# A new order of steps over five engines, the last experts in column halves, and products of ones ahead of the first queries

## The chip, the cores and the metric

The kernel runs on one core of a Trainium2 chip. The metric is the device time of one execution in microseconds (us), the median of three runs. The profile is one further execution, taken by the hardware profiler.

## The reference

Attention that keeps the 32 largest scores of each row, and behind it a mixture of four experts, all in float32. Batch 2, 8 heads, 576 positions, head width 64; 1152 tokens of width 512; four experts of inner width 1024.

```python
scores = q @ k.T / sqrt(64)
kth = 32nd largest of each row of scores
attn = softmax(where(scores >= kth, scores, -1e9))
x = (attn @ v), heads side by side            # 1152 x 512
p = domain_probs / domain_probs.sum(-1)
out = sum over e of p[:, e] * (relu(x @ w1[e]) @ w2[e])
```

## The kernel before

**Tiles and units.** The tokens are cut into ten tiles t0 to t9 of 128 rows (t0 and t9 have 64 rows). A unit u is one head of a tile (in t0 and t9 one pair of heads): t0 holds u0 to u3, t1 u4 to u11, and so on, eight a tile; t5 holds u36 to u43, t6 u44 to u51, t9 u68 to u71. Every float32 operand of the large products is split into a high and a low float16 half, and a product is three float16 products.

**The way of a unit.** `emit_qk` (L642) makes the scores of a unit in PSUM, in one of two buffers. Seven VectorE steps (`topk_op`, MAX8 at L655 and MATCH_REPLACE8 at L657 and L659) find the 32nd largest score. `emit_nb` (L692, L695) makes the bias of the exponential, `emit_exp` (L699) the exponential on ScalarE, and `emit_mask` drops what is below the threshold, either in one VectorE operation (mode d, L706) or in two on ScalarE and one on GpSimd (mode r, L709, L713, L716). `emit_a` splits the weights into halves (L724 on ScalarE, L726 and L728 on GpSimd), `emit_at` transposes them by a DMA from SP's queue (L734, tile `at`), and `emit_av` (L764) multiplies them with v.

**The way of a tile.** When its units are done, `emit_x_half` normalises (L784 to L788), `x_hi` and `x_lo` split x (L808 on ScalarE, L813 on GpSimd), a DMA transposes it (L816, tile `xt`), and `moe` runs the experts: `m1` (L881 to L883, half an expert's inner width at a time), ReLU and split (`h_hi` L892, `h_lo` L899 and L906, or L902 on VectorE), `m2` (L924), and `evac`, which adds an expert's result into the accumulator `o`, on VectorE (L948) or by ScalarE and GpSimd (L946, L951). The accumulator is stored by one DMA a tile (L955). In t9 experts go in pairs, each on 64 columns of the array, so two matmuls run side by side.

**The start.** Queries of t0 are loaded and transposed (L558), keys transposed (L579), and the first scores are float32 products (L598). `kv_gram` and `w_gram` (L1027, L497) are matmuls from which scales are found; the weights come in sixteen DMAs of 1 MB (`load_w`, L341) and are scaled and split on ScalarE and GpSimd (L526, L532, L535).

**What sets the order.** Every step is registered under an index, and the table `ISSUE` gives each stage of each step its place in one sequence. The five engines execute in exactly that order, so an instruction that waits holds back all that stand behind it on its engine. The strings `H_LO`, `MASKS`, `NB`, `EVAC` and `KV1` choose the engine of single steps (a is ScalarE, d VectorE, p GpSimd, r the mask in three operations). `MASKS` and `NB` have one letter a unit, u0 first.

Of the kernel before, what the change touches and what calls it, by code (L numbers as in the profile page):

```python
# [9 lines left out]
BF16 = mybir.dt.bfloat16  # L10
# [33 lines left out]
H_LO = ('pddd', 'dppppppp', 'pppppppd', 'dpdpppdp', 'dppppppp', 'pppdpdpp', 'pppppdpp', 'pppppppp', 'pppppppp', 'ppdp')  # L44

MASKS = 'ddddddddddddddddrrrrrrrrrrrrrrdrrdrrrrrrrrrdrdrrrrrrrrrrrrrrrrrrrrrrrrrr'
NB = 'aaaapdpadddaaadddddpdddadddpdddpdpapadppppppppaaaaadpppapppaapppppapaapp'
# [6 lines left out]
EVAC = ('dddp', 'dppd', 'dddd', 'dppd', 'ddpp', 'dppp', 'dddd', 'dddd', 'dddd', 'dddd')  # L54
KV1 = dict(k='aaaaaaad', v='aaaaaaaa')
# [1166 lines left out]
```

## Time and profile before

| | us |
|---|---|
| median of three runs | 544.7 |
| lowest and highest | 543.14, 544.88 |
| device time of the profiled execution | 546.72 |
| its span, first to last instruction | 544.9 |
| TensorE busy | 504.1 |
| VectorE busy | 432.0 |
| ScalarE busy | 368.3 |
| GpSimd busy | 366.1 |

The execution falls into a stretch in which VectorE has no gaps and TensorE has many (from about 10 to 110 us), one in which both are nearly full (110 to 310), one in which TensorE is full but for a few waits (310 to 400), one in which it is full (400 to 540), and the 4.9 us behind the last matmul. Busy time of TensorE takes the latency of a matmul in, so gaps below that don't show in it. The granted clock is shown as a share of the full 2.4 GHz; for the first 12 us the profile has no record of it, and the durations of equal instructions tell it there.

### The profile page before, as it was taken

How to read it: one execution, taken by the hardware profiler on the slowest of the kernel's cores; microseconds unless marked ns; L12 is line 12 of the kernel's file. 1: busy time of each engine (PE TensorE's matmuls, PEld its weight loads, DVE VectorE, ACT ScalarE, POOL GpSimd, SP SyncE). 2: the span in 40 equal slices, each digit the busy share in tenths (PEclk: the TensorE clock that was granted, in tenths of full speed). 3: DMA queues.
4: the chain of work that ended last, by engine and by line, in shares of the span. 5: the costliest groups of instructions: out<-in, count | busy, mean ns of one | idle time of the engine just before them, and what ended most of it. 6: DMA issues, size and time to landing. Idle time of an engine off the chain costs nothing.

```text
span 544.9 us, 16191 instructions
## 1 busy us (share of the span) xinstructions
PE 504.1 (93%) x6666; PEld 379.9 (70%) x6666; DVE 432.0 (79%) x965; ACT 368.3 (68%) x604; POOL 366.1 (67%) x404
## 2 busy tenths in 40 slices
PE   5978875699999999999999989999999999999996
PEld 3657754586777677868777767767867686777584
DVE  3999999999999999999999887987897877600111
ACT  2999999998777777688877566666655574234121
POOL 0599999998887767686977666685864764445210
PEclk9977996999999999999999989999999999999999
DMA  7999997543443645655524752354323232201300
GB/s 174 358 260 325 248 298 165 101 92 79 88 93 59 147 76 109 136 93 102 121 68 88 122 89 64 66 72 66 65 45 77 47 69 47 43 2 27 69 4 30
DMA packets 142698, 58.35 MB, mean 107 GB/s; under 512 B 130080, under 2 KB 134304, under 8 KB 142624
## 3 DMA queue, kind: packets, MB, share of 16 engines
q1 hardware_dynamic: 139200, 54.43, 46.9%
q10 hardware_dynamic: 3424, 2.88, 1.7%
q8 instruction: 52, 0.85, 0.6%
q14 instruction: 22, 0.18, 0.1%
HBM read 25.45 MB, written 2.36 MB: 51 GB/s over the span
## 4 chain that ended last, share of the span: by engine, by line
PE 53%; DVE 16%; POOL 9%; DMA 7%; issue 7%; ACT 7%; SPq 1%; POOLq 0%; ACTq 0%; DVEq 0%
PE m L924 23%; DVE m L655 7%; PE m L881 7%; PE m L882 7%; PE m L883 7%; DMA at<-a 4%; DVE w L659 3%; PE ps L642 3%; PE av L764 3%; POOL a L726 3%; DVE w L657 2%; POOL w L716 2%; DVE w L706 1%; POOL h L906 1%; ACT w L699 1%
## 5 line engine op out<-in xcount | busy, mean ns | idle before, releaser
L883 PE MATMUL m<-xt,w 128*128 128x128 f16 (+1 forms) x1280 | 198.8, 215 | 0.5 <-POOL w L535 0.5
L924 PE MATMUL m<-w,h 128*128 128x512 f16 (+1 forms) x960 | 196.0, 379 | 0.2 <-ACT o L943 0.2
L881 PE MATMUL m<-xt,w 128*128 128x128 f16 (+1 forms) x1120 | 177.8, 214 | 1.2 <-DMA xt<-xhl 1.2
L882 PE MATMUL m<-xt,w 128*128 128x128 f16 (+1 forms) x1120 | 177.8, 214 | 0.0
L655 DVE MAX8 m<-w 128x8 f32<-128x576 f32 x216 | 161.2, 754 | 3.1
L924 PEld LDWEIGHTS <-h 128*128 128x128 f16 (+1 forms) x960 | 84.0, 100 | 89.9 <-issue 1.1
L883 PEld LDWEIGHTS <-w 128*128 128x128 f16 x1280 | 123.2, 98 | 0.6 <-POOL w L535 0.6
L881 PEld LDWEIGHTS <-w 128*128 128x128 f16 x1120 | 108.0, 98 | 4.4 <-issue 2.5
L906 POOL TENSOR_TENSOR h<-hf,h 128x512 f16<-128x512 f32 x59 | 68.5, 1161 | 62.4 <-ACT hf L899 57.9
L882 PEld LDWEIGHTS <-w 128*128 128x128 f16 x1120 | 107.7, 98 | 1.8
L659 DVE MATCH_REPLACE8 w<-m,w 128x576 f32<-128x576 f32 x144 | 106.9, 742 | 0.0
L726 POOL TENSOR_TENSOR a<-w,a 128x512 f16<-128x512 f32 x68 | 79.0, 1162 | 31.0 <-ACT a L724 26.1
L716 POOL TENSOR_TENSOR w<-w,d 128x576 f32<-128x576 f32 x52 | 66.7, 1287 | 34.0 <-ACT d L713 30.1
L892 ACT ACTIVATE h<-m 128x512 f16<-128x512 f32 x72 | 42.7, 593 | 61.5 <-PE m L883 40.2
L699 ACT ACTIVATE w<-ps,nb,es 128x576 f32<-128x576 f32 x68 | 56.3, 828 | 31.6 <-DVE m L655 27.3
L655 DVE MAX8 m<-ps 128x8 f32<-128x576 f32 x72 | 54.6, 758 | 27.5 <-PE ps L642 16.5
L948 DVE SCALAR_TENSOR_TENSOR o<-m,pniw,o 128x512 f32<-128x512 f32 (+1 forms) x17 | 12.6, 744 | 62.4 <-PE m L924 51.9
L724 ACT ACTIVATE a<-w 128x576 f16<-128x576 f32 x68 | 45.8, 679 | 19.1 <-POOL w L716 12.9
L657 DVE MATCH_REPLACE8 w<-m,ps 128x576 f32<-128x576 f32 x72 | 53.8, 747 | 0.0
L642 PE MATMUL ps<-kt,qa 128*128 128x288 f16 x128 | 35.5, 296 | 16.5 <-DVE w L706 11.5
L764 PEld LDWEIGHTS <-at 128*128 128x128 f16 (+1 forms) x1008 | 36.3, 100 | 12.9 <-DMA at<-a 7.5
L764 PE MATMUL av<-vt,at 128*128 128x65 f16 (+1 forms) x1008 | 39.5, 195 | 5.6 <-DMA at<-a 5.6
(159 smaller groups left out, 769.3 us busy)
## 6 DMA issues: line engine op xcount, KB each, us to landing
w<-in_moe_w_dram SPq DMA_DIRECT2D x16, 1024.0 KB, 7.7
qraw<-in_q_dram SPq DMA_DIRECT2D x8, 256.0 KB, 3.5
qb<-qa SPq DMA_DIRECT2D x16, 128.0 KB, 2.5
out_dram<-o ACTq DMA_DIRECT2D x8, 256.0 KB, 2.7
at<-a SPq DMA_TRANSPOSE x68, 3.3
vraw<-in_v_dram SPq DMA_DIRECT2D x2, 512.0 KB, 7.8
nraw<-in_v_dram SPq DMA_DIRECT2D x4, 256.0 KB, 3.2
kraw<-in_k_dram SPq DMA_DIRECT2D x4, 256.0 KB, 2.9
```

Source lines behind the costliest of these rows:

```text
L655: DVE.max(m, s_t[u] if r == 0 else w_t[u])
L657: DVE.match_replace(rows2(w_t[u]), m, s_t[u], NEG)
L659: DVE.match_replace(w_t[u], m, w_t[u], NEG)
L699: ACT.activation(rows2(w_t[u]), s_t[u], AF.Exp, bias=nb, scale=es)
L716: POOL.tensor_tensor(w, w, g, op=OP.mult)
L726: POOL.tensor_tensor(a[:, 640:1152], w[:, 0:512], a[:, 0:512], op=OP.subtract)
L764: PE.matmul(o, lhsT=att[:, blk, ps], rhs=r, start=(i == 0), stop=(i == len(seq) - 1))
L881: PE.matmul(o, lhsT=HI[e, 0, c][:, fc], rhs=xs(0, c), start=(c == 0), stop=False)
L882: PE.matmul(o, lhsT=HI[e, 0, c][:, fc], rhs=xs(1, c), start=False, stop=False)
L883: PE.matmul(o, lhsT=LO[e, 0, c][:, fc], rhs=xs(0, c), start=False, stop=(c == 3))
L906: POOL.tensor_tensor(h[:, 1], hf, h[:, 0], op=OP.subtract)
L924: PE.matmul(y[z * 64:z * 64 + M, :], lhsT=h_t[es, qd][:, p // 2, h0:h0 + M], rhs=w, start=(fc == 0 and p == 0), stop=(fc == 7 and p == 2))
```

## The change

Four things are changed.

- The table `ISSUE` is replaced: all steps are the same, their sequence is another one on all engines. 
- The letters of `H_LO`, `MASKS`, `NB`, `EVAC` and `KV1` are others. Of 68 units behind t0, masks in one VectorE operation are 20 instead of 16.
- In t9, `m2` of the last pair of experts goes over the columns in two halves of 256. The first half stays in the bank of `m2`, the second goes to the bank that `av` had. `evac` adds each half by VectorE operations on 256 columns, and each half is stored by a DMA of its own, the first from SP's queue, the second from ScalarE's.
- Ahead of everything else TensorE gets 24 matmuls of ones with ones (bf16, 128 by 128) into the bank `m2`; nothing reads the result.

```diff
-H_LO = ('pddd', 'dppppppp', 'pppppppd', 'dpdpppdp', 'dppppppp', 'pppdpdpp', 'pppppdpp', 'pppppppp', 'pppppppp', 'ppdp')
+H_LO = ('pddd', 'dppppppp', 'ppppdppp', 'dpppppdp', 'dpdpppdp', 'ppppdppd', 'pppppppp', 'pppppppp', 'pppdpppp', 'pppp')
-MASKS = 'ddddddddddddddddrrrrrrrrrrrrrrdrrdrrrrrrrrrdrdrrrrrrrrrrrrrrrrrrrrrrrrrr'
-NB = 'aaaapdpadddaaadddddpdddadddpdddpdpapadppppppppaaaaadpppapppaapppppapaapp'
+MASKS = 'ddddddddddddddddrrdrrrrrrrrdrrrrrrrrrrrdrdrrrrdrrrrdrrdrrrrrrdrrrrrrrrrr'
+NB = 'aaaadddddddaddadddddaadaadaapdddpppapppdpaaapapaaappppppapppppappaaaaaaa'
-EVAC = ('dddp', 'dppd', 'dddd', 'dppd', 'ddpp', 'dppp', 'dddd', 'dddd', 'dddd', 'dddd')
-KV1 = dict(k='aaaaaaad', v='aaaaaaaa')
+EVAC = ('ddpp', 'ddpp', 'dddp', 'ddpp', 'dppp', 'dpdd', 'dddd', 'dddd', 'dddd', 'dddd')
+KV1 = dict(k='aaaaadaa', v='aaaaaaaa')
 ISSUE = [
-    (1,), (9,), (10,), (42,), (48,), (0, 3), (2, 4), (23, 24), (43, 47), (27, 31), (14,), (15, 16), (19, 22, 35, 41),
...
             def m2(es, qd):
                 if qd == 0:
                     y_t[es] = bank(ps_m2, "m2")
+                    if t == tiles[-1] and es[-1] == order[-1]:
+                        y2_t.append(bank(ps_av, "av"))
...
+                    if t == tiles[-1] and es[-1] == order[-1]:
+                        continue
...
+                if t == tiles[-1] and es[-1] == order[-1]:
+                    for hc in (slice(0, 256), slice(256, 512)):
+                        for f in range(4):
+                            fc = qd * 4 + f
+                            for p in range(3):
+                                for z, e in enumerate(es):
+                                    h0 = (4 * z + f) * M
+                                    w = (LO if p == 1 else HI)[e, 1, fc // 2]
+                                    w = w[:, (fc % 2) * 512 + hc.start:(fc % 2) * 512 + hc.stop]
+                                    PE.matmul((y2_t[0] if hc.start else y)[z * 64:z * 64 + M, hc], lhsT=h_t[es, qd][:, p // 2, h0:h0 + M], rhs=w,
+                                              start=(fc == 0 and p == 0), stop=(fc == 7 and p == 2))
...
+                if t == tiles[-1] and es[-1] == order[-1]:
+                    r0 = t[0] * S + t[1]
+                    for hc, zs in ((slice(0, 256), (0,)),) if z == 0 else ((slice(0, 256), (1,)), (slice(256, 512), (0, 1))):
+                        for zz in zs:
+                            DVE.scalar_tensor_tensor(
+                                acc[0][0:M, hc], (y2_t[0] if hc.start else y_t[es])[zz * 64:zz * 64 + M, hc], pniw[0:M, group(t), es[zz]:es[zz] + 1],
+                                acc[0][0:M, hc], op0=OP.mult, op1=OP.add)
+                        if z == 1:
+                            (ACT if hc.start else SP).dma_start(out=out[r0:r0 + M, hc], in_=acc[0][0:M, hc])
+                    yield
+                    yield
+                    return
...
         DVE.memset(ones, 1.0)
         DVE.memset(kraw0[64:128, 4], 0.0)
+        warm = bank(ps_m2, "m2")
+        for _ in range(24):
+            PE.matmul(warm[:, 0:128], lhsT=ones.bitcast(BF16)[:, 0:128], rhs=ones.bitcast(BF16)[:, 0:128], start=True, stop=True)
```

Three places show what the sequence does. The first is SP's queue at the start. `kraw0`, `vraw0`, `qraw` are keys, values and queries, `pn` the probabilities, `w00` and `w10` the first weights of experts 0 and 1, `qa` the transposed queries of t1. Before:

```order
L976 DMA kraw0_143<-in_k_dram 128x4x64 x4
L356 DMA qraw_204<-in_q_dram 128x8x64
L1006 DMA pn_120<-in_moe_domain_probs_dram 128x4x4
...
L341 DMA w00_123<-in_moe_w1_dram 128x2x1024 x2
...
L341 DMA w10_125<-in_moe_w1_dram 128x2x1024 x2
L393 DMA_TRANSPOSE qa_440<-qhl_206 128x8x128
```

And of the change:

```order
L1004 DMA kraw0_143<-in_k_dram 128x4x64 x4
L357 DMA qraw_254<-in_q_dram 128x8x64
L342 DMA w00_123<-in_moe_w1_dram 128x2x1024
L1037 DMA pn_120<-in_moe_domain_probs_dram 128x4x4
...
L342 DMA w00_123<-in_moe_w1_dram 128x2x1024
...
L342 DMA w10_125<-in_moe_w1_dram 128x2x1024
L394 DMA_TRANSPOSE qa_398<-qhl_258 128x8x128
L342 DMA w10_125<-in_moe_w1_dram 128x2x1024
```

The first half of `w00` moves ahead of the probabilities, and the second half of `w10` behind the transpose of the queries, which waits for GpSimd.

The second place is TensorE around u46 and u47, the third and fourth head of t6, one row of each block of matmuls. `ps0` are scores (the row with `kt6` is u50), `av` the products with v, `at` the transposed weights of a unit. Before, u47 (`at_5789`) and then u46 (`at_5929`):

```order
L642 MATMUL ps0_5848<-kt6_137,qa_4140 128x288
L764 MATMUL av_5727<-vt_139,at_5789 128x65
...
L881 MATMUL m1_5880<-xt_5719,wx0_129 128x128
...
L642 MATMUL ps0_5942<-kt7_138,qa_4140 128x288
...
L924 MATMUL m2_5756<-w31_1110,h_5703 128x512
...
L764 MATMUL av_5727<-vt_139,at_5929 128x65
```

And of the change, u46 (`at_5860`) and later u47 (`at_6031`):

```order
L643 MATMUL ps0_5864<-kt6_137,qa_4402 128x288
...
L882 MATMUL m1_5875<-xt_5783,wx0_129 128x128
...
L765 MATMUL av_5746<-vt_139,at_5860 128x65
...
L929 MATMUL m2_5798<-w31_908,h_5718 128x512
...
L643 MATMUL ps0_5973<-kt7_138,qa_4402 128x288
...
L882 MATMUL m1_5980<-xt_5783,w00_123 128x128
...
L765 MATMUL av_5746<-vt_139,at_6031 128x65
```

Before, the product of u47 stands right behind the scores of u50; now an `m1` block stands between these scores and u46, and an `m2` block, scores and another `m1` block between u46 and u47.

The third place is VectorE at the end of the program, where `o` is the accumulator of t9, `m2` and `av` the two banks of results. Before:

```order
L948 SCALAR_TENSOR_TENSOR o_9467<-m2_9418,pniw_121,o_9467 64x512
L948 SCALAR_TENSOR_TENSOR o_9467<-m2_9571,pniw_121,o_9467 64x512 x2
```

And of the change:

```order
L976 SCALAR_TENSOR_TENSOR o_9576<-m2_9428,pniw_121,o_9576 64x512
L961 SCALAR_TENSOR_TENSOR o_9576<-m2_9588,pniw_121,o_9576 64x256 x2
L961 SCALAR_TENSOR_TENSOR o_9576<-av_9589,pniw_121,o_9576 64x256 x2
```

The last two additions of 512 columns have become four of 256, two on each bank.

## Rows read from the trace of the kernel before

**Rows 1.** Stretches: us; busy us (instructions) PE, PEld, DVE, ACT, POOL; clock; DMA share; GB/s.

```profile
10.00:110.00 100.00, 75.75 (x1156) 61.54 (x1154) 98.13 (x255) 94.33 (x121) 87.67 (x68) 0.88 0.95 248
110.00:310.00 200.00, 198.07 (x2506) 149.56 (x2504) 192.41 (x425) 154.36 (x278) 153.04 (x183) 1.00 0.49 97
310.00:400.00 90.00, 85.83 (x1070) 65.17 (x1069) 75.22 (x156) 57.58 (x100) 60.16 (x69) 0.98 0.42 72
400.00:540.00 140.00, 139.97 (x1928) 101.14 (x1924) 63.74 (x125) 59.45 (x102) 64.22 (x73) 1.00 0.22 42
540.00:544.90 4.90, 0.00 (x0) 0.00 (x0) 1.50 (x2) 0.00 (x0) 0.00 (x0) 1.00 0.12 27
...
323.20:326.60 3.40, 3.40 (x36) 3.40 (x34) 2.57 (x5) 1.04 (x2) 1.56 (x3) 0.50 0.00 0
```

**Rows 2.** Waits: TensorE, 10 to 110 us; us in total, times, longest.

```profile
PE ps L642 <- DVE w L706: 11.5, 7, 2.8
```

**Rows 3.** Waits: TensorE, 110 to 540 us.

```profile
PE av L764 <- DMA at<-a: 3.4, 3, 2.4
PE m L881 <- DMA xt<-xhl: 1.2, 1, 1.2
PE ps L642 <- ACT d L709: 0.9, 3, 0.5
```

**Rows 4.** Timeline: start, duration, engine, line; in brackets idle before and what ended it.

```profile
322.23 0.61 PE L764 MATMUL av<-vt,at 128*128 128x65 f16 x14 [2.37 <-DMA at<-a]
```

**Rows 5.** Timeline: TensorE at the first `m1` of t6.

```profile
368.18 0.22 PE L881 MATMUL m<-xt,w 128*128 128x128 f16 x1 [1.19 <-DMA xt<-xhl]
```

**Rows 6.** Chain that ended last: start, duration of one half expert of `m2`.

```profile
348.93 2.59 PE m L924 x12
```

**Rows 7.** Timeline: TensorE and VectorE, 0 to 24 us.

```profile
0.82 0.17 DVE L996 MEMSET ones<- 128x128 f32 x1 [0.82 <-PEq L1209]
...
5.14 0.66 PE L558 MATMUL m<-ident,qraw 64*128 64x64 f32 x4 [5.14 <-DMA qraw<-in_q_dram]
...
7.54 2.19 PE L598 MATMUL ps<-kf,qf 64*64 64x288 f32 x8 [0.39 <-ACT kf L572]
...
9.66 2.32 PE L1027 MATMUL m<-kraw 128*128 128x128 bf16 x20
9.77 0.77 DVE L655 MAX8 m<-ps 128x8 f32<-128x576 f32 x1 [7.98 <-PE ps L598]
...
14.42 1.19 PE L598 MATMUL ps<-kf,qf 64*64 64x288 f32 x8
```

**Rows 8.** Groups by line: instructions, busy us, mean ns, idle before.

```profile
L695 DVE TENSOR_SCALAR nb<-m,es 128x1 f32<-128x1 f32 x20 | 3.9, 199 | 0.0
```

**Rows 9.** The same view: VectorE additions and products on 128 and 512 columns.

```profile
L503 DVE SCALAR_TENSOR_TENSOR m<-m,ident 128x128 f32<-128x128 f32 x8 | 2.3, 288 | 0.2 <-PE m L497 0.2
...
L948 DVE SCALAR_TENSOR_TENSOR o<-m,pniw,o 64x512 f32<-64x512 f32 x3 | 2.2, 749 | 17.0 <-ACT o L943 10.3 <-PE m L924 6.7
```

**Rows 10.** Timeline: the end of the program.

```profile
534.60 5.37 PE L924 MATMUL m<-w,h 128*64 128x512 f16 x48
...
540.02 1.53 DVE L948 SCALAR_TENSOR_TENSOR o<-m,pniw,o 64x512 f32<-64x512 f32 x2 [6.67 <-PE m L924]
541.58 0.53 ACTq L955 DMA_DIRECT2D out_dram<-o  x1
```

**Rows 11.** DMA issues: count, KB each, median us from issue to landing.

```profile
w<-in_moe_w_dram SPq DMA_DIRECT2D x16, 1024.0 KB, 7.7
...
qb<-qa SPq DMA_DIRECT2D x16, 128.0 KB, 2.5
...
qb<-qa SPq DMA_DIRECT2D x2, 64.0 KB, 2.3
```

**Rows 12.** Timeline: SP's queue, the second weights and the transpose of the queries.

```profile
16.66 1.72 SPq L341 DMA_DIRECT2D w<-in_moe_w_dram  x2
24.32 1.36 SPq L393 DMA_TRANSPOSE qa<-qhl  x1
```

More of the change, by code (lines that the diff above doesn't have):

```diff
@@ L828, in moe @@
             M = 64 if rest else 128
-            h_t, y_t = {}, {}
+            h_t, y_t, y2_t = {}, {}, []
             acc = [None]
```

316 rows, old and new, of the table ISSUE are left out of this document.

## The prediction

> **What bounds the kernel now.** I read the stretches first, then TensorE's waits, then the timeline at the few places where they lie. The reader is to see three things. From 10 to 110 us VectorE is busy for 98.13 of 100 us and TensorE for 75.75 [rows 1]; the largest of TensorE's waits there, 11.5 us in seven, is for the VectorE mask that gives a score buffer back [rows 2]. So up to 110 us the top-k steps set the pace. From 110 to 540 us TensorE is the bound: it is busy for 198.07 of 200, 85.83 of 90 and 139.97 of 140 us [rows 1]. Its idle time there is 1.93 + 4.17 + 0.03 = 6.13 us. In 3.4 us of that stretch the granted clock is 0.50, the lower of its two levels [rows 1]; 36 matmuls that run at half rate lose half of it, 1.7 us. So 7.8 us of the full stretch can be won by a better order, no more, since matmuls are neither removed nor made shorter there. Of the idle time 3.4 + 1.2 = 4.6 us are waits for transposing DMAs, 0.9 for ScalarE [rows 3]. Behind the last matmul come 4.9 us [rows 1].
>
> VectorE is close to full from 110 to 310 us as well (192.41 of 200 [rows 1]), so an order that asks it for more ahead of a unit can turn into a new wait there.
>
> **The start.** The products of ones can begin when the ones are written, 0.82 + 0.17 = 1.0 us [rows 7]. Their price is bounded by the 20 bf16 matmuls of the same size that took 2.32 us early in the program [rows 7]: 24 x 2.32 / 20 = 2.8 us, so they end at 3.8 us. The first transposes start at 5.14, on the landing of the queries [rows 7]. So the products cost nothing; without that cover of 1.3 us they would cost up to 2.8. What they may bring is the clock. Eight float32 score matmuls took 2.19 us at 7.54 and 1.19 us at 14.42 [rows 7]: TensorE ran at the lower level at the first and at the upper at the second. VectorE had nothing to do until 9.77 and waited for exactly these [rows 7]. At the upper level the first MAX8 comes 1.0 us earlier by them alone, and a little more by the transposes ahead, which also take less. Those are held in part by the landing of the last keys, so I take 1.3 us; the bounds are 0 (the clock has not risen, or has fallen back in the pause) and 1.6.
>
> The Trainium skill says in "TensorE: Matmul & The Clock Gate", Part 1, that the lower level is the default, that sustained activity releases it and idling brings it back. By that rule the products help only if they last long enough and the pause behind them is short enough; the trace has no such pair of burst and pause. By the rule the first MAX8 would stay at 9.77. This is one of the rivals below.
>
> What VectorE gains at its start it keeps only if it is asked for no more on its way to 110 us. From 10 us on it has almost no gap, so instructions can be counted. The score buffer that TensorE waits for last in that stretch is freed by the mask of u12. By the letters of `NB`, biases on VectorE ahead of it are nine (u4 to u10, u12, u13) instead of five (u5, u8, u9, u10, u14): four more, each 0.199 us [rows 8], +0.8 us. The top-k steps, masks and sums ahead of it are the same number. Net: -1.3 + 0.8 = **-0.5 us** at the point where TensorE becomes full. Bounds: -0.8 if the clock gives 1.6, +0.8 if it gives nothing.
>
> SP's queue costs nothing as long as the weights arrive in time: the first half of `w00` moves ahead by four small DMAs, the second half of `w10` moves behind the transpose of the queries, which waits for GpSimd. The price, if that cover is gone, stands with the rivals.
>
> **The full stretch.** The longest wait is 2.37 us at 322.23, for the transposed weights of u47 [rows 4]; the low clock from 323.20 to 326.60 follows on that idle time. So this one place costs 2.4 + 1.7 = 4.1 us. The change puts an `m1` block, the product of u46, an `m2` block, scores and a further `m1` block between the scores of u50 and that product. The `m2` block alone takes 2.59 us [rows 6], more than the wait. So the wait and the low clock go, unless the transpose itself comes later by as much; GpSimd and ScalarE, which feed it, are not full there (60.16 and 57.58 of 90 us [rows 1]). What is late next at 368.18 is the first `m1` of t6, which waited 1.19 us for its transposed x [rows 5]. The new order puts one more product ahead of it, 0.4 us or so; I give no gain for it.
>
> The other waits, 6.13 - 2.37 = 3.8 us, are spread over many places. The sequence is another one everywhere, the transposes stand in another order in SP's queue, and VectorE and TensorE are both within 4% of full up to 310 us. Some of these waits go and others come. I take them as equal; the bounds are 3.8 us less (no waits at all) and 4.1 us more (one more place like that at 322 us). The letters of the strings move work between VectorE, ScalarE and GpSimd; from 110 us on this lies beside full matmuls and costs nothing, as long as no score buffer is late. Sum for the stretch: **-4.1 us**.
>
> **The end.** The 48 matmuls of 512 columns took 5.37 us [rows 10], two side by side on halves of the array. 96 of 256 columns stream as many columns; I take no loss. The trace has no such matmuls with 256 columns; if every one of them cost 10 ns more than half of one before, it would be +0.5 us. The first column half is complete a quarter of the block ahead of the end, 1.3 us, and its two additions lie beside the matmuls of the second. Behind the last matmul stand two additions on 256 columns instead of two on 512, which took 1.53 us [rows 10]. One on 128 columns takes 0.288, on 512 0.749 [rows 9]; in between, 0.288 + (0.749 - 0.288) / 3 = 0.44, an estimate. Two make 0.88, **-0.6 us**. The last store is 64 KB instead of 128. For other transfers of these sizes the landing took 2.3 and 2.5 us [rows 11], so it brings 0.2 at most, and I take nothing.
>
> The Trainium skill advises against two transfers in place of one: "DMA: Bandwidth & Descriptors", Rules for kernel authors, says of disjoint halves of the partitions that they serialize on the same engines. Here the halves are columns, and the first store is issued about 0.9 us ahead. By that rule nothing is won by the smaller store, which is the value taken.
>
> **The sum.** -0.5 - 4.1 - 0.6 = -5.2 us. The profiled execution has a span of 544.9 and a device time of 546.72 us; the median of the runs is 544.7, 2.0 below that device time. I take the difference over to the median: 544.7 - 5.2 = 539.5 us.
>
> **Rivals.**
>
> - *The clock does not rise in time.* For it speaks the pause of 1.3 us. The start is then +0.8 instead of -0.5: 540.8 us. Chance 0.2.
> - *Waits change places.* The place at 322 us is relieved, and its 4.1 us come back at others, since the order is new everywhere and VectorE is 96% busy up to 310 us. For it: a queue of transposes on SP serves all units, and what one unit gains in time another loses. Against: the largest single part of TensorE's loss there, 4.1 of 7.8 us, sits in one place, and that one is plainly relieved. 544.7 - 0.5 - 0.6 = 543.6 us. Chance 0.19.
> - *Nearly all waits go.* If the order leaves slack behind every transpose, 7.8 us go, with the start and the end: 544.7 - 7.8 - 0.5 - 0.6 = 535.8 us. Chance 0.16.
> - *Slower: the second weights come late.* SP issued both halves of `w10` at 16.66 us and the transpose of the queries at 24.32 [rows 12]. Now the second half waits behind that transpose. If this stays at 24.32, the half is issued at 24.32 + 1.36 = 25.7 and lands, by the median of these loads, 7.7 us later [rows 11], at 33.4. The matmuls on it stand ahead of the first scores of t1 on TensorE, which VectorE needs by then. The delay is between 0 (ScalarE and GpSimd prepare the queries some 4 us earlier) and about 6; at 3 us, with the biases and no gain from the clock or in the full stretch, 544.7 + 3 + 0.8 - 0.6 = 547.9 us. It decides when VectorE shows a gap of over 2 us ahead of t1. Chance 0.1.
> - The change does what it says in any case: the columns and the products are written out.
>
> **How the numbers follow.** The forecast, 539.5, has the remaining 0.35. A measurement of this kernel can tell 0.3%, 1.6 us, from no change. Faster by more, below 543.1: the forecast, the clock rival, nearly all waits, and a quarter of the exchange, 0.35 + 0.2 + 0.16 + 0.05 = 0.76, less 0.04 for a combination of small losses: 0.72. Within 0.3%: the rest of the exchange, 0.14, and 0.03 of that 0.04, so 0.17. Slower: the slow rival and the last 0.01, so 0.11. The range reaches from 535.3 (nearly all waits go, and 0.5 us more from the bounds of the clock and the store) to 544.7, the exchange with a start that brings nothing; it leaves out the slow rival and a part of the small losses.
>
> **What would show it.** Right: the score matmuls at some 6 to 7 us take 1.2 us and the first MAX8 starts near 8.5; the first full stretch begins about half a us earlier; no wait of TensorE over 1 us and no low clock between 110 and 540 us; two VectorE additions of 0.4 us behind the last matmul. Wrong: scores still at 2.2 us; a new wait of 2 us or more with the clock at 0.50 behind it; a gap on VectorE between 25 and 40 us; matmuls of the last block that take longer than 5.4 us.

## The result

| | before | changed |
|---|---|---|
| first comparison, median us | 544.75 (542.97 to 546.91) | 539.9 (537.42 to 542.99) |
| ratio, 95% interval | | 0.9917 (0.9896 to 0.9938) |
| the same kernel later, two other comparisons | 544.91 and 544.84 | 538.08 and 538.4 |
| ratios there | | 0.9873 (0.9849 to 0.9897), 0.9899 (0.9863 to 0.9935) |
| profiled execution: device time, span | 546.72, 544.9 | 540.16, 538.4 |

The forecast was 539.5 with faster as the likeliest sign; the first comparison gave 539.9. The sum was met, its terms were not: the start brought nothing that can be told, the full stretch brought more than forecast, and of the place at 322 us on which the forecast rested another execution of the kernel before shows only 0.45 us.

Stretches of the changed kernel, with the columns of [rows 1]:

```profile
10.00:110.00 100.00, 75.21 (x1119) 61.23 (x1118) 95.62 (x253) 92.11 (x116) 84.09 (x63) 0.88 1.01 245
110.00:310.00 200.00, 198.64 (x2537) 150.71 (x2534) 192.99 (x425) 157.94 (x287) 159.56 (x187) 1.00 0.54 101
310.00:400.00 90.00, 90.00 (x1120) 67.39 (x1118) 83.92 (x172) 57.03 (x98) 57.26 (x72) 1.00 0.39 71
400.00:535.00 135.00, 134.21 (x1937) 100.51 (x1933) 60.09 (x119) 55.30 (x98) 59.48 (x64) 1.00 0.22 39
```

From 310 to 400 us TensorE has no idle time left, against 4.17 us in [rows 1], and the clock is 1.00 in every stretch from 110 us on. What is missing in the last row, 0.79 us, lies behind the last matmul. In the first row VectorE is busy for 2.5 us less than before: it waited.

TensorE's waits, 110 to 535 us, that answer to [rows 3]:

```profile
PE ps L643 <- DVE w L707: 0.8, 1, 0.8
PE m L882 <- DVE h L903: 0.5, 1, 0.5
```

No wait for a transposing DMA is among them; before there were 4.6 us of those. The first row is the wait ahead of the scores of u16 at 111.41, where the full stretch begins.

The time can be cut at two points that every trace shows: the first score matmul of u16, from which on TensorE is full, and the first of the two VectorE additions that stand last. For the kernel before and the changed one, the first point and the second:

```profile
108.53 0.30 PE L642 MATMUL ps<-kt,qa 128*128 128x288 f16 x1 [1.61 <-DVE w L706]
```

```profile
111.41 0.30 PE L643 MATMUL ps<-kt,qa 128*128 128x288 f16 x1 [0.77 <-DVE w L707]
...
534.25 1.00 DVE L961 SCALAR_TENSOR_TENSOR o<-av,pniw,o 64x256 f32<-64x256 f32 x2 [0.31 <-PE av L940]
```

Before, the second point is at 540.02 [rows 10]. From the first MAX8 to u16 TensorE does 1135 matmuls in both orders (rows further down), so the three parts can be compared, and so they can in the traces of all experiments:

| trace | to u16 | full stretch | end | span |
|---|---|---|---|---|
| before | 108.53 | 431.5 | 4.9 | 544.9 |
| before, again (e9) | 111.41 | 428.9 | 4.9 | 545.2 |
| before, two products later (e6) | 109.05 | 429.6 | 4.9 | 543.6 |
| changed | 111.41 | 422.8 | 4.1 | 538.4 |
| changed, again (e8) | 108.98 | 423.2 | 4.1 | 536.3 |
| changed, third (e12) | 108.18 | 423.0 | 4.1 | 535.3 |
| without products (e1) | 108.77 | 422.8 | 4.1 | 535.7 |
| 36 products (e2) | 109.14 | 423.0 | 4.1 | 536.2 |
| whole columns at the end (e3) | 108.73 | 422.9 | 4.96 | 536.6 |
| one `m2` block later (e4) | 108.65 | 422.8 | 4.1 | 535.6 |
| order and letters alone (e5) | 111.65 | 422.8 | 4.9 | 539.3 |
| start mended (e7) | 114.17 | 422.8 | 4.1 | 541.1 |
| one load later (e10) | 110.05 | 423.35 | 4.1 | 537.5 |
| no products, load later, probabilities early (e11) | 110.81 | 423.1 | 4.1 | 538.0 |

The reader is to see that with the new order the full stretch is 422.8 to 423.35 us in eleven traces, whatever came ahead of it, and with the old one 428.9 to 431.5 in three; that the end is close to one of two values, 4.1 or 4.9; and that nearly all that still differs between executions of the changed kernel lies ahead of u16.

### The profile page after: what moved, and what is told of

Its sections match the earlier page's. It is cut to its first block, busy times and chain, and to the rows that moved or that the text cites. A ratio compares the mean times of both kernels' runs of the same rounds, so it can differ in the third digit from the quotient of the medians.

```text
span 538.4 us, 16332 instructions
## 1 busy us (share of the span) xinstructions
PE 505.1 (94%) x6738; PEld 384.6 (71%) x6738; DVE 433.7 (81%) x969; ACT 365.0 (68%) x602; POOL 361.4 (67%) x397
## 4 chain that ended last, share of the span: by engine, by line
PE 78%; DVE 14%; DMA 2%; ACT 2%; SPq 2%; issue 1%; POOL 0%; DVEq 0%
PE m L929 34%; PE m L882 11%; PE m L883 11%; PE m L884 11%; DVE m L656 6%; PE av L765 5%; PE ps L643 5%; DVE w L660 3%; DVE w L658 2%; DVE w L707 2%; DMA at<-a 2%; DMA pn<-in_moe_domain_probs_dram 1%; ACT w L533 1%; ACT w L527 1%; PE m L940 1%
## 5 line engine op out<-in xcount | busy, mean ns | idle before, releaser
L929 PE MATMUL m<-w,h 128*128 128x512 f16 (+1 forms) x912 | 191.4, 383 | 0.0
L929 PEld LDWEIGHTS <-h 128*128 128x128 f16 (+1 forms) x912 | 81.6, 101 | 88.4 <-issue 2.2
L883 PEld LDWEIGHTS <-w 128*128 128x128 f16 x1120 | 108.5, 99 | 1.6
L717 POOL TENSOR_TENSOR w<-w,d 128x576 f32<-128x576 f32 x48 | 61.4, 1282 | 27.6 <-ACT d L714 27.5
L900 ACT ACTIVATE hf<-m 128x512 f32<-128x512 f32 x59 | 34.9, 591 | 7.5 <-POOL h L907 6.0
```

Of the source, the lines that this page charges most:

```text
L717: POOL.tensor_tensor(w, w, g, op=OP.mult)
L883: PE.matmul(o, lhsT=HI[e, 0, c][:, fc], rhs=xs(1, c), start=False, stop=False)
L929: PE.matmul(y[z * 64:z * 64 + M, :], lhsT=h_t[es, qd][:, p // 2, h0:h0 + M], rhs=w, start=(fc == 0 and p == 0), stop=(fc == 7 and p == 2))
```

## The experiments

**The parts of the change, taken away one by one.** Without the products (e1):

```diff
-        warm = bank(ps_m2, "m2")
-        for _ in range(24):
-            PE.matmul(warm[:, 0:128], lhsT=ones.bitcast(BF16)[:, 0:128], ...)
```

> The changed kernel without its 24 products of ones; all else as there. In the changed kernel's profile the score matmuls at 7.73 us took 2.18 us and the first MAX8 came at 9.96, as late as before (9.77), so my theory now is that the products bring nothing but an earlier rise of the clock behind the scores (11.84 instead of 12.58). It expects: score matmuls 2.2 us, first MAX8 at 9.8 to 10.0, the later matmuls of the first 12 us at the lower level, and a time equal to the changed kernel's within 0.8 us (539.9). The rival, that the products are worth something later in the start, expects 0.8 to 1.5 us more, 540.7 to 541.4, and a clock that rises 0.7 us later.

Measured: 537.73 us (536.67 to 538.43), ratio 0.9874 (0.9842 to 0.9905). The changed kernel itself had 0.9873 to 0.9917. The time is 2.2 us below the 539.9 of the first comparison, more than the 0.8 that the theory allowed, but within 0.7 us of the two later comparisons. So the products are worth nothing that can be measured; the rival, that they bring 0.8 us or more, falls. Score matmuls of u0 took 2.18 us, as with the products in the changed kernel's three traces.

With 36 products (e2):

```diff
-        for _ in range(24):
+        for _ in range(36):
```

> The changed kernel with 36 products of ones instead of 24. At 0.114 us each they end at 5.15 us instead of 3.78, so the pause of 1.56 us ahead of the first transposes at 5.34 all but goes. If the pause was what kept the clock low, the score matmuls take 1.2 us instead of 2.18, the first MAX8 comes at 8.9 instead of 9.96, and the time falls by about 1 us, to 538.9. The rival, that what matters is the length of the work from 5.3 us on or that the pause is no matter, expects score matmuls of 2.2 us, the first MAX8 at 9.9 and no gain: 539.9 within 0.8.

Measured: 539.08 us (536.24 to 539.68), ratio 0.9891 (0.9859 to 0.9923). The clock did rise in time: score matmuls in 1.19 us, the first MAX8 at 8.61 instead of 9.96. That part of the expectation holds. The time is near the 538.9 that was expected, but the changed kernel itself had 538.1 to 539.9, so it doesn't tell; the trace does, since the scores of u16 still came at 109.14. Where the gain went is shown below.

With whole columns at the end (e3, the `m2`, `evac` and store of the last pair as before), and with order and letters alone (e5, also without the products):

> The changed kernel with the last pair of experts in whole columns again (48 matmuls of 512 columns, two additions of 512 columns, one store), order and products as changed. Theory: the halves are worth what stands behind the last matmul, 4.9 us before and 4.2 now; so 0.7 us more than the changed kernel, 540.6, with two VectorE additions of 1.53 us in all behind the last matmul and a block of 5.37 us. Rival (the smaller additions are eaten up by slower matmuls or by the second store): no difference, 539.9, and no more than 4.3 us behind the last matmul.

> The changed kernel without the products of ones and with the last pair of experts in whole columns again: what is left of the change is the order and the letters. In the traces so far, of four kernels with this order, the time from the scores of u16 to the last block of matmuls is 420.0 to 420.1 us, against 428.7 before, whatever the start did; the scores of u16 came at 108.65 to 111.41, against 108.53. Theory: the order alone gives nearly all: 8.7 us less behind u16, nothing at the start, so 537.5 to 539.0, about 0.7 above the run without products (537.7). Rival (order, products and halves each carry a part): 540 or more.

Measured: e3 540.35 us (537.93 to 543.97), ratio 0.9929 (0.9898 to 0.996); e5 540.86 us (537.89 to 541.98), ratio 0.9914 (0.9886 to 0.9941). The medians are drowned in what differs ahead of u16; the traces are not: the end is 4.9 to 5.0 us in both, against 4.1 to 4.15 in every trace with halves. So the halves give 0.8 us, and order and letters together the rest: 422.8 us for the full stretch in e5 too. No run has the new order with the old letters, so the two are not told apart. The time of e3 is the one that its theory gave. That of e5 fits its rival, 540 or more; the trace speaks against the rival, since the loss lies ahead of u16, at 111.65, as in the trace of the unchanged e9. That the other five executions of e5 lost their time there too is not shown.

**The place at 322 us.** The kernel before with the two products moved by one block each (e6), and the kernel before unchanged, for its trace (e9):

```diff
+ISSUE[894] = (1620,)    # was 1608: av of u47
+ISSUE[887] = (1636,)    # was 1628: av of u46
```

> The kernel before with two products moved by one block each on TensorE: that of u47 behind the m1 block that followed it, that of u46 behind the next m1 block. This is the single place on which the forecast's -4.1 us rested (wait of 2.37 us at 322.23 and the low clock behind it, 1.7 us). By the forecast's step: no wait there, no low clock at 323 to 327, and 4.1 us less than before on the same chip, about 540.1. Rival one (waits change places): the products or the m1 blocks behind wait for other transposed weights instead, and the gain is under 1.5 us. Rival two (the place is no more than a part of the loss): 1.5 to 3 us.

> The kernel before once more, one look at its trace. The run with the products of u47 and u46 moved showed no wait and no low clock around 322 us, and 1.9 us less from the scores of u16 to the last block than the first trace of before (426.8 against 428.7), yet its time did not differ from before's (ratio 1.000). Theory: the wait of 2.4 us with the low clock behind it belonged to the profiled execution, which was 2.0 us above the median of before, and isn't there in most; then this trace shows a wait of under 1 us for the transposed weights of u47, no low clock between 300 and 350 us, and 426 to 427.5 us from the scores of u16 to the last block. Rival: the wait is always there and other waits take its place when it is removed; then this trace shows 2 us or more at u47, the low clock behind, and 428 to 429.

Measured: e6 545.39 us (544.03 to 547.23), ratio 1.0004 (0.9984 to 1.0023), no gain at all. The product of u47 in e9, and the stretch around it there (columns of [rows 1]):

```profile
324.27 0.61 PE L764 MATMUL av<-vt,at 128*128 128x65 f16 x14 [0.45 <-DMA at<-a]
```

```profile
310.00:350.00 40.00, 39.47 (x526) 30.83 (x526) 36.70 (x79) 27.27 (x49) 29.73 (x33) 1.00 0.47 86
```

Without any change the wait was 0.45 us instead of 2.37 [rows 4], with no low clock behind it. What differed is how long the transpose of u47 took from issue to landing (start and duration in the chain that ended last, first trace of before, then e9):

```profile
316.89 5.29 DMA at<-a
```

```profile
320.84 3.39 DMA at<-a
```

The two differ by 1.90 us, the waits by 1.92. The theory of e9 holds at this place: all but 0.45 of the 4.1 us belonged to the profiled execution. Why the transpose took longer there is open. The full stretch of e9 is 2.6 us shorter than in the first trace, not 4.1, since other waits were longer there or new (1.5 us in three for ScalarE instead of 0.9 [rows 3], 0.6 for the queries). Two of the waits of e9, 112 to 535 us:

```profile
PE ps L642 <- ACT d L709: 1.5, 3, 1.2
...
PE m L881 <- DMA xt<-xhl: 1.0, 1, 1.0
```

Not every wait of before was of one execution only. The first `m1` of t6 waited 1.19 us in the first trace [rows 5], 0.98 in e9 and 1.31 in e6, and its transpose landed in 4.9 to 5.3 us each time; in the changed kernel's three traces it landed in 3.2 to 3.3, and nothing waited.

**The start.** One `m2` block behind the products that VectorE waits for (e4), three places at once (e7):

```diff
+ISSUE[1173] = (383,)    # e4: was 364, m2 of the first pair in t0, first half
```

```diff
+ISSUE[29] = (76,)       # e7: was 35 on VectorE, sums of the probabilities
+ISSUE[1173] = (397,)    # e7
-        for _ in range(24):
+        for _ in range(36):
```

> The changed kernel with one block moved: the first half of the first pair's m2 in t0 goes on TensorE behind the product of u4, the second matmuls of the scales of experts 3 (w1) and the product of u7, instead of ahead of them. In the changed kernel's profile VectorE stands idle for 3.55 us at 82.2 to 85.7, for a scale whose matmul stands behind that block (4.07 us at the lower clock), which stands behind a product that waited 3.2 us for its transposed weights. Theory: this gap is why TensorE becomes full 2.9 us later than before the change (scores of u16 at 111.4 against 108.5); so the gap falls to 1 us or less, the scores of u16 come 2 to 3 us earlier, and the time is 537 to 538. Rival: the gap is only where VectorE waits for ScalarE and GpSimd, which are full from 45 to 80 us; then it moves elsewhere and the time stays at 539.9 within 0.8.

> The changed kernel with 36 products of ones (end at 5.1 us, behind them no pause), with the sums of the probabilities on VectorE 14 instructions later (behind the last step of u1), and with the first half of the first pair's m2 in t0 behind the product of u4, the scale of expert 3 and the scores of u13. With 36 products alone the first MAX8 came at 8.61 instead of 10.13, but VectorE gave 1.2 us of it back at the probabilities, which land later than before, 1.2 us more right behind, and the rest at 83 us, where it waits for a matmul. Theory: these three joints are where the gain of the clock goes; with all three relieved the first scores come 1.3 to 2 us earlier, VectorE has no gap over 0.6 us up to 110, the scores of u16 come at 106.5 to 107.5, and the time is 535.5 to 537. Rival: ScalarE and GpSimd, which are full from 45 to 80 us, set the time of u16; then it stays at 108.5 or later and the time at 537.5 to 540.

> The changed kernel once more, on the chip of the other three, for the spread of its times (so far 537.4 to 543.0 us; the version without products 536.7 to 538.4 in six runs). If the products, which raise the clock early in some executions and not in others, make the spread, this one spreads over 4 us or more and the two without products (the order alone, and the earlier run) over 2 or less. If the spread comes from DMA landings that differ from execution to execution, the order alone spreads as widely. Its time: 538 to 541.

Measured: e4 540.88 us (537.37 to 543.84), ratio 0.9924 (0.9894 to 0.9954); e7 541.01 us (539.96 to 542.96), ratio 0.9926 (0.9902 to 0.995), beside 538.08 us (536.14 to 539.99) of the unchanged e8 on the same chip. Both theories fall. The traced execution of e4 did what its theory said (u16 at 108.65, 537.37 us), but it is the fastest of twelve, and e8 came to 108.98 without the move. That of e7 came to 114.17. With e5's spread of 4 us the idea that the products make the spread falls too.

What the traces show instead is a start with several joints, at each of which VectorE waits for something that its own early work does not hasten. From the first MAX8 to u16 VectorE is busy for 96.8 to 98.7 us in all fourteen traces; the rest of that time is idle: 1.9 us in the first trace of before, 4.8 in e9, 4.4, 1.8 and 1.3 in the changed kernel's three, 3.4 in e4 and 7.4 in e7. In e4 the clock rose in time and the first MAX8 came at 8.11. VectorE's rows of e4 for the sums of the probabilities and the scores of u13:

```profile
14.71 0.20 DVE L1042 TENSOR_REDUCE psumr<-pn 128x10 f32<-128x40 f32 x1 [1.25 <-DMA pn<-in_moe_domain_probs_dram]
...
85.73 0.77 DVE L657 MAX8 m<-ps 128x8 f32<-128x576 f32 x1 [1.39 <-PE ps L644]
```

1.25 us go at the probabilities, whose four small DMAs now stand behind the first half of `w00` on SP; 1.39 us go at 85.73, where in e1, without any products, the same instruction stood at 85.74. Together this is more than the 1.85 us by which its first MAX8 was earlier than the changed kernel's. The rival of e4 and e7, that ScalarE and GpSimd set the time of u16, is not excluded: every wait of VectorE over 0.3 us from the first MAX8 to u16 ends, in all fourteen traces, on TensorE or on a transfer, none on these two, but they feed both, and GpSimd is busy for 49.5 of the 50 us from 40 to 90 in the changed kernel's first trace.

And the clock falls back. The durations of the eight score matmuls of u0 to u3, with the pause between the products and the first transposes:

| trace | pause us | u0 | u1 | u2 | u3 |
|---|---|---|---|---|---|
| before | | 2.19 | 1.19 | 1.19 | 1.19 |
| e9 | | 2.19 | 1.19 | 1.19 | 1.19 |
| e6 | | 2.18 | 1.19 | 1.19 | 1.19 |
| e1 | | 2.18 | 1.19 | 1.19 | 1.19 |
| e5 | | 2.19 | 2.18 | 1.19 | 1.19 |
| e11 | | 2.18 | 2.18 | 1.19 | 1.19 |
| changed | 1.56 | 2.18 | 1.19 | 1.19 | 1.19 |
| e8 | 1.62 | 2.19 | 2.18 | 1.19 | 1.19 |
| e12 | 1.40 | 2.18 | 1.19 | 1.19 | 1.19 |
| e3 | 1.35 | 2.18 | 2.18 | 1.19 | 1.19 |
| e10 | 1.33 | 2.19 | 1.19 | 1.19 | 1.19 |
| e4 | 1.15 | 1.19 | 2.18 | 1.19 | 1.19 |
| e7 | 0.35 | 1.19 | 2.18 | 1.19 | 2.18 |
| e2 | none | 1.19 | 1.19 | 2.18 | 1.19 |

In each of the three traces in which u0 was fast, a later one was slow. Six starts have the same 24 products from 1.04 to 3.78 us, and in one of them, e4, the clock rose early: it was granted in full from 4.41 us on, within the pause, ahead of the first transpose at 4.93. So that the shorter pause decided is not shown. In e7 TensorE waited 0.52 and 0.99 us for keys around u0, and the transposes and scores behind ran at the lower level (granted clock 1.00 from 4.5 to 11.1 us, 0.50 from 11.25 to 18.0); the second of these waits:

```profile
9.30 1.13 PE L1060 MATMUL m<-kraw 128*128 128x128 bf16 x17 [0.99 <-DMA kraw<-in_k_dram]
```

The Trainium skill, "TensorE: Matmul & The Clock Gate", Part 1, has idling bring the lower level back; these rows agree, and in e2, e4 and e7 a rise that came early was lost again by 19.2, 11.2 and 11.2 us.

**The joint at 80 us.** One weight load behind the transpose for u6 instead of ahead of it (e10), and that without products and with the probabilities early (e11):

```diff
+ISSUE[1575] = (335.5,)  # was 316: first half of w2 of expert 3, on SP
+ISSUE[28] = (16,)       # e11: was 26, DMAs of the probabilities, on SP
```

> The changed kernel with one weight load moved on SP: the first half of the w2 of expert 3, which stands as the last of three ahead of the transpose of the weights of u6, goes right behind it. In two of seven traces of this order TensorE waited 2.4 and 3.2 us at 77 to 80 us for that transpose, the clock fell, the m2 block behind took 4.07 us instead of 2.8, and VectorE stood for 2.8 and 3.6 us; in the others the wait was 0.4 to 1.1 us and no such gap followed. Theory: this landing makes the spread of 537 to 543 us; with a load less ahead of it the wait is under 1 us in nearly all executions, so the times lie within 3 us and the median is 537 to 538.5. Rival: the landing does not depend on that load, or the load then comes late for its own matmuls at 89 us; then spread and median stay those of the changed kernel on the same chip.

> The changed kernel without products of ones, with the load moved as in the run beside it, and with the four small DMAs of the probabilities ahead of the first weights again, as in the kernel before. The products brought nothing by the time of u16 in any trace, and VectorE waited up to 1.25 us for the probabilities at 13 to 15 us. If landings ahead of 90 us are all that is left of the start, the scores of u16 come at 108 to 109 and the time is 536.5 to 538, with a spread of 2 to 3 us. Rival: neither is the cause, and the time is that of the changed kernel on the same chip, within 1 us.

> The changed kernel a third time, as the measure for the two runs beside it on the same chip. Theory (landings at 77 to 80 us decide): times in two groups, near 537.5 and near 541 to 543, with a median between 538 and 540.5; behind the scores of u16 again 420.0 to 420.4 us to the last block.

Measured: e10 539.43 us (538.65 to 540.97), ratio 0.9909 (0.9881 to 0.9936); e11 539.11 us (538.38 to 540.3), ratio 0.9902 (0.9875 to 0.9929); e12 538.4 us (537.12 to 542.65). Neither e10 nor e11 beats the changed kernel, measured beside them as e12. In e10 the times lie within 3 us as its theory said, but the median is above its 537 to 538.5; e11 missed both its time and u16 (110.81); the seven times of e12 have the median that was expected, but no two clear groups (537.1 to 538.5 five times, 540.33, 542.65). TensorE and VectorE in the changed kernel's first trace:

```profile
79.81 0.76 PE L765 MATMUL av<-vt,at 128*128 128x65 f16 x14 [3.21 <-DMA at<-a]
...
80.87 4.07 PE L929 MATMUL m<-w,h 128*64 128x512 f16 x24
...
85.33 0.36 PE L507 MATMUL m<-gd,ones 128*128 128x1 f32 x2
...
85.72 0.16 DVE L280 TENSOR_SCALAR wpt<-m 128x1 int32<-128x1 int32 x1 [3.55 <-PE m L507]
```

and TensorE in e12:

```profile
77.62 0.62 PE L765 MATMUL av<-vt,at 128*128 128x65 f16 x14 [0.62 <-DMA at<-a]
...
78.44 2.78 PE L929 MATMUL m<-w,h 128*64 128x512 f16 x24
```

The clock in the changed kernel's block (columns of [rows 1]):

```profile
80.20:83.40 3.20, 3.20 (x22) 1.73 (x20) 1.97 (x6) 2.81 (x6) 3.20 (x3) 0.50 0.85 175
```

In this trace one landing decides: late, it costs the wait, then the lower level in the block behind (4.07 us instead of 2.78), and VectorE stands for 3.55 us at a scale whose matmul comes after that block. In e5 it was the same wait, with 2.81 us on VectorE. The old order has the like: in e9 TensorE waited 2.79 us at 75.78 for a weight load, the clock fell, VectorE stood for 2.75 us at 78.92, and u16 came at 111.41. In e10 the wait for u6 was gone and another had come, 1.65 us at 82.88 for the transposed weights of u4, whose transpose now stands closer behind the moved load; that the load made it late is not shown. So late landings account for most of the difference between u16 at 108 to 109 and u16 at 111 to 112 in these three traces. For e7, e10 and e11, whose idle time is spread over several waits, that is argued and not shown. Which transfer is late differs from execution to execution, and how to remove these waits is open.

## Why the prediction came out

**The start, forecast -0.5, measured about 0.** The term of the clock, -1.3, failed first: its rival was right in all three traces of the changed kernel (first MAX8 at 9.8 to 10.0 us). The step behind it, "What VectorE gains at its start it keeps only if it is asked for no more on its way", lacked a condition. Where the clock did rise (e2, e4, e7), 1.3 to 1.9 us at the first MAX8 could not be told at u16 any more (109.14, 108.65), or had turned into a loss (114.17 in e7), though VectorE's work was nearly the same. The argument took VectorE, without gaps in the trace of before, for the bound; it was, only as long as nothing it needs came later. Unit u16 came at 108.5, 111.4 and 109.05 in the three traces with the start of before, and at 111.4, 109.0 and 108.2 in those of the changed kernel: no difference can be told.

**The four biases, forecast +0.8, measured +0.8, net of other steps +0.2.** VectorE's busy time from the first MAX8 to u16, of before and then of the changed kernel (columns of [rows 1]):

```profile
9.77:108.53 98.76, 74.51 (x1135) 60.40 (x1135) 96.89 (x253) 92.86 (x120) 86.20 (x66) 0.88 0.95 249
```

```profile
9.96:111.41 101.45, 75.89 (x1135) 61.80 (x1135) 97.07 (x255) 93.52 (x118) 85.50 (x63) 0.88 1.01 243
```

Two instructions more, not four, and 0.18 us. Nine biases instead of five do stand there, 1.80 us instead of 0.99; but two reciprocals of scales, 0.28 us in all, now stand behind u16, so the other steps, which the sum had taken as equal in number, are not, and the rest of the difference lies in overlaps of short instructions. The mask that frees the buffer for u16 is the fifteenth in both traces, that of u14 and not of u12 as the prediction has it; the count of nine to five holds for it.

**"SP's queue costs nothing".** For the weights that held: the second half of `w10` was issued at 21.87 us, since the transpose of the queries came at 20.46 instead of 24.32 [rows 12], and in the first trace of the changed kernel VectorE had no gap over 0.2 us between 10 and 80. The slower rival did not come, for the reason that the prediction gave as its lower bound. For the probabilities, which now stand behind the first half of `w00`, it failed: VectorE waited 1.25 us for them in e4, and 0.7 to 0.9 in e5, e10 and e12, where the clock was not early.

**The full stretch, forecast -4.1, measured -8.6 between the two traces, and -6 against the second trace of before.** Two steps failed, in opposite directions. The place at 322 us was taken from one execution as a property of the kernel; e9 shows that nine tenths of it are not, and e6 gained nothing by moving it. And the other waits were taken "as equal", where nearly all of them went, those that stand in every trace of before among them: for the 1.19 us at the first `m1` of t6 [rows 5] the prediction gave no gain. That nearly all waits go was a rival, with a chance of 0.16 and 7.8 us. Its reason, slack behind every transpose, could have been counted: from the issue of a unit's transpose on SP to its product on TensorE it is 3.3 us at least and 7.05 in the median before (from 110 us on), and 5.1 and 8.2 in the changed kernel; from the transpose of a tile's x to its first `m1`, 3.0 to 3.9 us for six of the eight tiles t2 to t9 before, 5.2 to 6.5 for all of them now. How long such a transpose takes to land, of before and 110 to 535 us (columns of [rows 11]):

```profile
at<-a SPq DMA_TRANSPOSE x59, 3.3
xt<-xhl SPq DMA_TRANSPOSE x8, 3.1
```

Nine of the 60 products from 110 us on began within 0.5 us of the landing of their weights, in the first trace of before and in e9, and none in the changed kernel's three traces. A landing that is later than usual is then a wait in the old order, and often none in the new one: in e2 the transpose for t7 landed in 4.9 us, and the 5.7 us that the new order leaves there took that in. So the gain came from several places of 0.2 to 1.3 us, some in every trace of before and some not, and not from the largest one. That the slack alone did it, and not the letters that move work off ScalarE, no run shows: the waits of 0.9 and 1.5 us for ScalarE are gone as well.

The bound of 7.8 us for the stretch was too low as well. A matmul's row lasts 0.22 us though the next begins 0.06 later, so the busy share hides idle time of up to 0.16 us at each gap. From start to start of successive matmuls, less the columns at full rate, the gaps over 0.12 us from u16 on sum to 8.1 us in the first trace of before, 7.0 in e9, and 1.2, 1.4 and 1.2 in the three of the changed kernel. The full stretch less these gaps, and less the 1.7 us of the low clock in the first trace, is 421.6 to 421.9 us in all five: the gaps and that one low stretch are the whole difference.

**The end, forecast -0.6, measured -0.8.** The two additions took 1.00 us, a little over the estimate of 0.88; the first two lay beside the matmuls, and the last block did not get slower (528.8 to 534.2, 5.4 us, as in [rows 10]). What is left of the end is 4.1 - 1.0 = 3.1 us against 4.9 - 1.5 = 3.4. This 0.3 us, which the prediction left out and bounded by 0.2, is the smaller last store: it landed 1.99 us after its issue, against 2.29. The rule of the Trainium skill, "DMA: Bandwidth & Descriptors", Rules for kernel authors, is on halves of the partitions; no run here has those, and with halves of the columns on two queues nothing of the kind shows: the first store, issued 1.3 us ahead of the second, landed in 1.99 us as well.

**The median.** The step that carried the difference of a profiled execution over to the median was the weak one. Both profiled executions of before (546.7 and 547.0) lie 2 us above its medians. Between them and the changed kernel's traces the spans differ by 6.5 to 9.9 us, the medians by 4.9, 6.8 and 6.4. The shorter full stretch of e9, 428.9, with the changed kernel's 423.0 gives 5.9, and with the end 6.7: that is what the later two comparisons measured. That the first came within 0.4 us of the forecast is part luck.

## What to carry to other kernels

Before a wait in a profile is taken for a property of the kernel, look whether a second execution has it, and how long it is there: here one of 2.37 us shrank to 0.45, and one of 1.19 came back with 0.98 and 1.31. Count the distance from issue to use for all transfers, against their landing, and compare old and new order by the smallest distances, not by the one wait that a trace happens to show; the small waits that stand in every trace are as much worth pricing. An engine without gaps keeps an earlier start only as far as the next point at which it needs another engine or a transfer; look for these points ahead of pricing the start.

## What the hardware showed that was not expected

The clock of TensorE was not a matter of warming up once. In the fourteen starts tabled above each group of eight score matmuls took either 1.19 or 2.18 to 2.19 us, nothing between, and one or two of the four groups were slow in all of them, with products ahead of the queries or without: where the clock rose ahead of u0, it was another group that was slow. The same group of the same kernel (u1 in the changed kernel and in e8) differed by 1 us for this reason alone. VectorE stood for 1.18 us behind it in e8, and yet the scores of u16 came at 108.98 there and at 111.41 in the first trace, where the one late landing at 80 us cost more.
